# Small state products as pairs of 64-column tiles in one run, eps rows over 128 rows, tail products in pairs of chunks

## Chip, cores, metric

One core of one Trainium2 chip. The metric is device time in microseconds (us) of one execution, the median of several runs. Instruction durations are in nanoseconds (ns) where marked.

## The reference, cut to what matters

Linear attention without softmax, an RMS norm per head, then a gated feed-forward layer.

```python
# q, k, v: (8 batches, 8 heads, 576 tokens, 64); g_norm: (64,)
kv  = einsum('bhsd,bhse->bhde', k, v)        # the "state": 64x64 per head
out = einsum('bhsd,bhde->bhse', q, kv)
attn = out / sqrt(mean(out*out, -1) + 1e-6) * g_norm
x = attn as (4608, 512)
xn = x / sqrt(mean(x*x, -1) + 1e-6) * rms_g
y = (silu(xn @ w_gate) * (xn @ w_val)) @ w_out   # 512 -> 1536 -> 512
```

Almost all the work is the feed-forward layer. The change concerns the small matmuls of the attention part, which stand in the same TensorE stream.

## The kernel before

Tokens are taken in nine groups: the first 512 tokens of each of the eight batches, and the eight tails of 64 tokens together ("tails"). In a group, `up` makes one of twelve units (four gate and four value matmuls of 512 columns, then a silu on ScalarE and a product on VectorE), and `down` makes output rows. While group n is in the feed-forward layer, the small products of group n+1 are put between its units.

The state of a pair of heads, before, for batches 2 to 7: one 128x128 product holds two heads, and its two off-diagonal 64x64 blocks are never read.

```python
def kv_pair(ps, b, j, first, last):
    if b < EARLY:                       # batches 0 and 1: 64x64 tiles
        ...
                PE.matmul(ps[rows, rows], lhsT=...[rows, j, c, :], rhs=...[rows, j, c, :], ...)
        return
    hs = slice(2 * j, 2 * j + 2)        # two heads: 128 columns
    for t in range(T + 1):              # T + 1 = 5 token blocks
        PE.matmul(ps, lhsT=bufs[b]["k"][:, t, hs, :], rhs=bufs[b]["v"][:, t, hs, :],
                  start=(first and t == 0), stop=(last and t == T))

# class Att
def kv_copy(self):                      # only the diagonal blocks are copied
    SC.copy(out=kv_all[0:D, n, :, 0:D], in_=ps[0:D, :, 0:D])
    DVE.tensor_copy(out=kv_all[D:128, n, :, D:128], in_=ps[D:128, :, D:128])
def o_products(self, c, ps):
    for j in range(NS):                 # NS = 4 head pairs
        cols = ps[:, 2 * j : 2 * j + 2, :]
        if self.tail:                   # two batches' tails of 64 rows in one chunk
            for u in range(2):
                rows = slice(u * TAIL, (u + 1) * TAIL)
                PE.matmul(cols[rows], lhsT=tails_q["t"][:, c, j, rows], rhs=kv_all[:, 2 * c + u, j, :], ...)
        else: ...                       # one full matmul
```

The schedule (`SC` is ScalarE):

```python
for n in range(1, B + 1):
    ...
    if n == 1:
        steps[0] += [lambda i=i: cast_kv(2, "k", i, DVE) for i in (2, 3)]
        steps[0] += [lambda i=i: cast_kv(2, "v", i, SC) for i in (0, 1)]
        steps[1] += [lambda i=i: cast_kv(2, "v", i, SC) for i in (2, 3)]
    if n < B:
        a = atts[n + 1]
        kv0, os = (2, (4, 5, 6, 7)) if n == 1 else (0, (2, 3, 5, 6))
        if not a.tail:
            steps[kv0] += [lambda a=a: a.kv_products((0, 1))]
            steps[kv0 + 1] += [lambda a=a: a.kv_products((2, 3)), a.kv_copy]
        for c, u in enumerate(os):
            steps[u].append(lambda a=a, c=c: a.o(c))
            ...
    for unit in range(NF + T):          # 12 up-units, 4 down-units
        ffn.up(unit) ...                # or down
        for step in steps[unit]: step()
```

`att_pool` has two PSUM banks. `A`, `Z` (halves of batch 0) and `F` (batch 1) make the sums of squares on TensorE: `sums` first puts eps into the bank by matmuls of `ones` (64 rows) with `epsrow` (64 rows), then adds `sel` matmuls of 128 rows and 4 columns.

Of the kernel before, what the change touches and what calls it, by code (L numbers as in the profile page):

```python
# [10 lines left out]
FP32 = mybir.dt.float32  # L11
BF16 = mybir.dt.bfloat16
# [8 lines left out]
def kernel(  # L21
# [14 lines left out]
    B, H, S, D = q.shape  # L36
# [5 lines left out]
    T = 4  # L42
    MAIN = 128 * T
    TAIL = S - MAIN
    NS = d_model // 128
# [7 lines left out]
    def pool(name, bufs, **kw):  # L53
        return ctx.enter_context(tc.tile_pool(name=name, bufs=bufs, **kw))

    consts = pool("consts", 1)
# [17 lines left out]
    att_pool = pool("att", 2, space=PS)  # L74
# [3 lines left out]
    PE, DVE, SC, GP = nc.tensor, nc.vector, nc.scalar, nc.gpsimd  # L78
# [5 lines left out]
    gsq = consts.tile([128, 1], BF16, name="gsq")  # L84
    rowscale = consts.tile([128, NS], FP32, name="rowscale")
    sel = consts.tile([128, 2, 2], BF16, name="sel")
    ones = consts.tile([64, 128], BF16, name="ones")
    epsrow = consts.tile([64, H], BF16, name="epsrow")
    gsq8 = consts.tile([128, H, D], BF16, name="gsq8")
    kv_all = consts.tile([128, B, NS, 128], BF16, name="kv_all")  # L90
    kbs = [consts.tile([128, T + 1, H, D], BF16, name=f"kb{i}") for i in range(2)]
# [21 lines left out]
    bufs = {b: {"k": kbs[b % 2], "v": vbs[b % 2]} for b in range(B)}  # L113
# [8 lines left out]
    def pairs_buf(b, name):  # L122
        flat = bufs[b][name].rearrange("p t h d -> p (t h d)")
        return flat[:, 0 : NS * C * D].rearrange("p (j c d) -> p j c d", j=NS, c=C)
# [19 lines left out]
    def cast_kv(b, name, i, engine):  # L144

        if b < EARLY:
            cast(engine, pairs_buf(b, name)[:, i].rearrange("p c d -> p (c d)"), pairs_raw(b, name)[:, i, :])
        elif i < NS:
            hs = slice(2 * i, 2 * i + 2)
            src = raws[b, name][:, 0 : MAIN * T].rearrange("p (h t d) -> p t h d", h=H, t=T)  # L150
            cast(engine, bufs[b][name][:, 0:T, hs, :], src[:, :, hs, :])
        else:
            src = raws[b, name][0:TAIL, MAIN * T :].rearrange("r (h d) -> r h d", h=H)
            cast(engine, bufs[b][name][0:TAIL, T], src)
# [10 lines left out]
    def alloc_q(b):  # L165
        bufs[b]["q"] = qb_pool.tile([128, T, H, D], BF16, name="qb")

    def cast_q(b, hs, engine):
        src = raws[b, "q"].rearrange("p (h t d) -> p t h d", h=H, t=T)[:, :, hs, :]
        cast(engine, bufs[b]["q"][:, :, hs, :], src)  # L170

    def load_batch(b):
        load_q(b)
        for name in ("k", "v"):
            alloc_kv(b, name)
            load_kv(b, name, nc.sync)
# [85 lines left out]
    def kv_pair(ps, b, j, first, last):  # L262
        if b < EARLY:
            for c in range(C):
                for u in range(2):
                    rows = slice(u * D, u * D + D)
                    PE.matmul(
                        ps[rows, rows], lhsT=pairs_buf(b, "k")[rows, j, c, :], rhs=pairs_buf(b, "v")[rows, j, c, :],
                        start=(first and c == 0), stop=(last and c == C - 1),
                    )  # L270
            return
        hs = slice(2 * j, 2 * j + 2)
        for t in range(T + 1):
            PE.matmul(  # L274
                ps, lhsT=bufs[b]["k"][:, t, hs, :], rhs=bufs[b]["v"][:, t, hs, :],
                start=(first and t == 0), stop=(last and t == T),
            )

    def clear_tail_rows(i, engine):

# [12 lines left out]
    class Att:  # L293
        def __init__(self, n):
            self.n = n
            self.tail = n == B
            self.outa = {}
            self.xna = {}
            self.sq = {}
            self.qt = None  # L300

        def kv_products(self, js):
            if js[0] == 0:
                self.kv_ps = att_pool.tile([128, NS, 128], FP32, name="att_ps")
            for j in js:
                kv_pair(self.kv_ps[:, j, :], self.n, j, j == 0, j == NS - 1)

        def kv_copy(self):
# [38 lines left out]
                        start=(j == 0), stop=(j == NS - 1),  # L347
                    )

        def o(self, c):  # L350
            ps = att_pool.tile([128, H, D], FP32, name="att_ps")
            self.o_products(c, ps)
            self.sq[c] = sq_pool.tile([128, 2, H, D], BF16, name="sq")
            SC.activation(out=self.sq[c][:, 0], in_=ps, func=ACT.Square)  # L354
            self.outa[c] = outa_pool.tile([128, H, D], BF16, name="outa")
            SC.copy(out=self.outa[c], in_=ps)  # L356
# [247 lines left out]
    eps_hi = float(ml_dtypes.bfloat16(eps))  # L604
    eps_lo = float(ml_dtypes.bfloat16(eps - eps_hi))
# [1 line left out]
    for i in range(2):  # L607
        DVE.memset(sel[i * D : (i + 1) * D, 0, i : i + 1], 1.0 / D)
    DVE.memset(ones, 1.0)
    DVE.memset(epsrow[0:32], eps_hi / 32)  # L610
    DVE.memset(epsrow[32:64], eps_lo / 32)
    DVE.memset(kv_all[:, 0 : B - 1], 0.0)


# [35 lines left out]
    def state0(j, dummies):  # L650
        ps = att_pool.tile([128, 512], FP32, name="att_ps")
        warm(ps, max(dummies, 1), 512 if dummies else 128)
        kv_pair(ps[:, 0:128], 0, j, True, True)
        return ps
# [38 lines left out]
    kv0 = state0(0, 0)  # L693
# [60 lines left out]
    first = ffn.pair_banks()  # L754
# [79 lines left out]
    att1 = Att(1)  # L834
# [46 lines left out]
    def down_part(c, lo, hi):  # L881
        ffn.down_products(c, lo, hi, pools[c])
# [4 lines left out]

    for c in range(4):
        down_part(c, 0, 2)
    att1.kv_products((0, 1, 2, 3))  # L890
    for i, engine in enumerate((DVE, SC)):
        cast_q(1, slice(2 * i, 2 * i + 2), engine)
    att1.kv_copy()
# [48 lines left out]
    def load_q_tails():  # L942
        st = stage().rearrange("p (c x) -> p c x", c=T)
        for b in range(B):
            u = b % 2
            nc.sync.dma_start(
                out=st[u * TAIL : (u + 1) * TAIL, b // 2].rearrange("r (h d) -> r h d", h=H),
                in_=q[b, :, MAIN:S, :].rearrange("h r d -> r h d"),
            )
        tails_q["raw"] = st  # L950
        tails_q["b"] = qb_pool.tile([128, T, H, D], BF16, name="qb").rearrange("p t h d -> p t (h d)")

    def cast_q_tails(c, n, engine):
        cast(engine, tails_q["b"][:, c : c + n], tails_q["raw"][:, c : c + n])
# [12 lines left out]
    for n in range(1, B + 1):  # L967
        ffn = Ffn(n)
        steps = {u: [] for u in range(NF + T)}
        if n + 2 < B:  # L970
            steps[2].append(lambda n=n: load_batch(n + 2))
        if n == B - 3:
            load_q_tails()
# [4 lines that stand above are left out]
            steps[0] += [lambda name=name: cast_kv(2, name, NS, GP) for name in ("k", "v")]  # L978
        if n < B:
            a = atts[n + 1]  # L980
            kv0, os = (2, (4, 5, 6, 7)) if n == 1 else (0, (2, 3, 5, 6))
            if not a.tail:
                steps[kv0] += [lambda a=a: a.kv_products((0, 1))]
                steps[kv0 + 1] += [lambda a=a: a.kv_products((2, 3)), a.kv_copy]
            for c, u in enumerate(os):
                steps[u].append(lambda a=a, c=c: a.o(c))
                steps[u + 1].append(lambda a=a, c=c: a.sums(c))
            late = 2 * int(n == 1)
            steps[8 + late] += [a.head]
            steps[9 + late] += [a.guess, a.root]  # L990
            for c in range(T):
                steps[10 if c == 0 and not late else 11] += [lambda a=a, c=c: a.scale(c), lambda a=a, c=c: a.x_rows(c)]
        b = n + 2
        if b < B:
            steps[10] += [lambda b=b: alloc_q(b)]
            for i in range(2):
                steps[11] += [lambda b=b, i=i: cast_q(b, slice(4 * i, 4 * i + 4), SC)]
            for i in KV_CASTS:
                steps[12 + i // 3] += [lambda b=b, i=i: cast_kv(b, "k", i, SC)]
                steps[14 + i // 3] += [lambda b=b, i=i: cast_kv(b, "v", i, SC)]  # L1000
            for c in range(T):
                steps[13].append(lambda b=b, c=c: atts[b].q_rows(c))
        if b == B:
            for i in range(2):
                steps[11] += [lambda i=i: cast_q_tails(2 * i, 2, SC)]
            for c in range(T):
                steps[13].append(lambda c=c: turn_q_tails(c))
        for unit in range(NF + T):
            if unit < NF:
                ffn.up(unit)  # L1010
            elif n == B and unit == NF + T - 1:
                ffn.down_last(unit - NF)
            else:
                ffn.down(unit - NF)
            for step in steps[unit]:
                step()
# [30 lines left out]
```

## Time and profile before

| | |
|---|---|
| time, median of 3 runs before the change was tried | 324.51 us (324.26 to 325.29) |
| span of the profiled execution | 323.5 us |
| PE busy | 313.6 us, 97% |
| chain that ended last | 86% PE |
| waits of PE for another engine or a load | 4.1 us, all before 48 us |

From the page of before: the span, the busy times (us, share of the span, instructions), and the shares of the chain that ended last.

```profile
span 323.5 us, 5112 instructions
PE 313.6 (97%) x1893; PEld 157.0 (49%) x1927; DVE 181.2 (56%) x371; ACT 178.9 (55%) x319; POOL 20.9 (6%) x43
PE 86%; DMA 6%; DVE 4%; issue 2%; ACT 1%; DVEq 0%
```

The second line alone doesn't prove that TensorE binds, since matmuls overlap. The chain does it, with the waits, and with the starts of the matmuls: from the first up-unit of batch 1 on, but for the tails' excursions to another tile shape (below), a matmul starts one stream time after the one before it, 216 ns after 512 columns and 56 ns after 128. A nanosecond less in that stream is a nanosecond less of time.

The groups of small matmuls, by form (line, engine, operation, rows x columns of the array and output shape, count, then busy us and mean ns of one, then idle time before them):

```profile
L274 PE MATMUL att_ps<-vb,kb 128*128 128x128 bf16 x120 | 8.7, 219 | 0.0
L340 PE MATMUL att_ps<-kv_all,qt 128*64 128x128 bf16 x32 | 1.7, 225 | 0.1
L418 PE MATMUL att_ps<-epsrow,ones 64*128 64x8 bf16 x8 | 0.7, 168 | 0.1
```

The 219 ns is the span of one matmul as the profile models it, not what it costs: the timeline shows the ten of a run within 0.72 us. What counts is the distance between starts. The timeline of before on PE around batch 3's state products (start us, duration of the merged piece, what):

```profile
90.90 1.03 PE L474 MATMUL v_ps<-xnt,wv_sb 128*128 128x512 bf16 x4
91.77 0.72 PE L274 MATMUL att_ps<-vb,kb 128*128 128x128 bf16 x10
92.32 1.03 PE L474 MATMUL g_ps<-xnt,wg_sb 128*128 128x512 bf16 x4
93.19 1.03 PE L474 MATMUL v_ps<-xnt,wv_sb 128*128 128x512 bf16 x3
94.05 0.72 PE L274 MATMUL att_ps<-vb,kb 128*128 128x128 bf16 x10
```

From 91.77 to 92.32 ten full matmuls take 0.56 us, and the gate matmuls follow at once. Now the tails' output products, which use half the columns of the array (128*64):

```profile
259.81 1.03 PE L474 MATMUL v_ps<-xnt,wv_sb 128*128 128x512 bf16 x4
260.76 0.41 PE L340 MATMUL att_ps<-kv_all,qt 128*64 128x128 bf16 x8
261.11 1.04 PE L474 MATMUL g_ps<-xnt,wg_sb 128*128 128x512 bf16 x4
262.94 0.41 PE L340 MATMUL att_ps<-kv_all,qt 128*64 128x128 bf16 x8
266.84 0.41 PE L340 MATMUL att_ps<-kv_all,qt 128*64 128x128 bf16 x8
269.02 0.41 PE L340 MATMUL att_ps<-kv_all,qt 128*64 128x128 bf16 x8
```

The last of four value matmuls starts at 259.81 + 3 x 0.216 = 260.45, so the tiles could start at 260.67; they start at 260.76. The single starts of that stretch, read from the trace:

```
start us   ns after the one before
260.453    216   last 512-column matmul
260.762    309   first tile of pair 1          (+93)
260.766      4   second tile of pair 1
260.842     76   pair 2                        (24 more than the next)
260.898     52   pair 3 (56 after pair 2)
260.954     52   pair 4
260.957      3
261.109    152   512-column matmul again       (+99: 155 after pair 4, which streams 56)
261.336    227   the next                      (+11)
```

An excursion to another tile shape and back thus costs 93 + 24 + 99 + 11 = 227 ns, about 0.23 us, apart from its work.

### The profile page before, as it was taken

What the parts mean: (1) busy time and instruction counts of PE and PEld (TensorE: products, weight loads), DVE (VectorE), ACT (ScalarE), POOL (GpSimd) and SP (SyncE); (2) the same over time, 40 slices, a digit from 0 to 9 for tenths busy, and PEclk for the clock granted to TensorE, in tenths of its full rate; (3) what the DMA queues carried; (4) which work ended last, traced back from release to release, by engine and by line L of the source; (5) the groups of instructions that cost most, each with busy time, mean ns of one, the idle gap of its engine ahead of it and who ended that gap; (6) DMA issues with size and microseconds to landing.
All of it is one profiled execution on the core that took longest, in us unless ns stands there. A gap on an engine that the chain in (4) does not pass through costs nothing.

```text
span 323.5 us, 5112 instructions
## 1 busy us (share of the span) xinstructions
PE 313.6 (97%) x1893; PEld 157.0 (49%) x1927; DVE 181.2 (56%) x371; ACT 178.9 (55%) x319; POOL 20.9 (6%) x43
## 2 busy tenths in 40 slices
PE   8899999999999999999999999999999999999995
PEld 3575455554454445544544455444544444444443
DVE  4776857569427932794278516950696068703310
ACT  3686447765757476647664766566554355223321
POOL 1253351200000000000000000000000000000000
PEclk9999999999999999999999999999999999999999
DMA  7999999888369449934792377947002600240014
GB/s 264 347 351 388 377 374 292 212 245 209 62 197 299 127 130 154 316 87 97 191 330 64 65 202 187 326 90 204 1 2 49 174 38 1 47 146 6 0 34 97
DMA packets 74437, 54.87 MB, mean 170 GB/s; under 512 B 42280, under 2 KB 67116, under 8 KB 74412
## 3 DMA queue, kind: packets, MB, share of 16 engines
q1 hardware_dynamic: 74044, 53.89, 58.2%
q10 hardware_dynamic: 368, 0.66, 0.6%
q8 instruction: 15, 0.25, 0.3%
q14 instruction: 10, 0.08, 0.1%
HBM read 37.75 MB, written 9.44 MB: 146 GB/s over the span
## 4 chain that ended last, share of the span: by engine, by line
PE 86%; DMA 6%; DVE 4%; issue 2%; ACT 1%; DVEq 0%
PE v_ps L474 26%; PE o_ps L516 26%; PE g_ps L474 26%; DMA st<-in_k_dram 3%; DMA st<-in_moe_w_gate_dram 3%; PE att_ps L274 2%; PE att_ps L345 2%; DVE h_sb L480 1%; DVE ssq L363 1%; PE v_ps L516 1%; PE g_ps L516 1%; DMA out_dram<-o_sb 1%; PE o_ps L491 1%; PE att_ps L340 0%; ACT wg_sb L202 0%
## 5 line engine op out<-in xcount | busy, mean ns | idle before, releaser
L480 DVE TENSOR_TENSOR h_sb<-silu,v_ps 128x512 bf16<-128x512 bf16 x104 | 70.9, 683 | 109.5 <-ACT silu L479 68.0
L474 PE MATMUL v_ps<-xnt,wv_sb 128*128 128x512 bf16 x409 | 105.7, 379 | 0.4
L474 PE MATMUL g_ps<-xnt,wg_sb 128*128 128x512 bf16 x401 | 104.9, 379 | 0.8 <-ACT wg_sb L202 0.2
L479 ACT ACTIVATE silu<-g_ps 128x512 bf16<-128x512 f32 x104 | 62.5, 601 | 64.2 <-PE g_ps L474 52.3
L516 PE MATMUL o_ps<-wo_sb,h_sb 128*128 128x512 bf16 x386 | 87.1, 379 | 0.5
L474 PEld LDWEIGHTS <-wv_sb 128*128 128x128 bf16 x416 | 40.7, 98 | 49.1
L516 PEld LDWEIGHTS <-h_sb 128*128 128x128 bf16 x420 | 40.7, 98 | 47.7
L474 PEld LDWEIGHTS <-wg_sb 128*128 128x128 bf16 x416 | 38.7, 98 | 39.9 <-issue 0.3
L106 ACT COPY o_sb<-o_ps 128x512 f32<-128x512 f32 (+1 forms) x34 | 19.7, 580 | 38.0 <-PE o_ps L516 32.4
L363 DVE TENSOR_REDUCE ssq<-sq 128x16 f32<-128x1024 bf16 x28 | 34.2, 1220 | 1.0
L354 ACT ACTIVATE sq<-att_ps 128x512 bf16<-128x512 f32 x28 | 16.7, 597 | 13.5 <-PE att_ps L345 7.9
L106 ACT CAST vb<-st 128x512 bf16<-128x512 f32 (+2 forms) x34 | 19.5, 626 | 4.8 <-DMA st<-in_v_dram 4.8
L380 DVE TENSOR_TENSOR xna<-outa,s1y 128x512 bf16<-128x512 bf16 x28 | 17.9, 684 | 0.0
L106 ACT CAST qb<-st 128x1024 bf16<-128x1024 f32 (+1 forms) x17 | 15.4, 943 | 1.8 <-DMA st<-in_q_dram 1.8
L356 ACT CAST outa<-att_ps 128x512 bf16<-128x512 f32 x28 | 16.2, 579 | 0.0
L106 ACT CAST kb<-st 128x512 bf16<-128x512 f32 (+1 forms) x25 | 14.0, 619 | 0.0
L362 DVE TENSOR_TENSOR sq<-sq,gsq 128x512 bf16<-128x512 bf16 x28 | 11.7, 418 | 0.0
L345 PEld LDWEIGHTS <-qt 128*128 128x128 bf16 x96 | 7.4, 98 | 5.7
L345 PE MATMUL att_ps<-kv_all,qt 128*128 128x128 bf16 x96 | 9.3, 219 | 0.1
L274 PEld LDWEIGHTS <-kb 128*128 128x128 bf16 x120 | 7.7, 98 | 2.8
L617 PE MATMUL att_ps<-kv_all 128*128 128x512 bf16 (+1 forms) x21 | 7.9, 504 | 1.2 <-DVE sel L606 1.2
L274 PE MATMUL att_ps<-vb,kb 128*128 128x128 bf16 x120 | 8.7, 219 | 0.0
(139 smaller groups left out, 166.5 us busy)
## 6 DMA issues: line engine op xcount, KB each, us to landing
out_dram<-o_sb SPq DMA_DIRECT2D x14, 512.0 KB, 3.0
st<-in_q_dram SPq DMA_DIRECT2D x6, 1024.0 KB, 6.7
st<-in_k_dram SPq DMA_DIRECT2D x6, 1024.0 KB, 9.4
st<-in_v_dram SPq DMA_DIRECT2D x6, 1024.0 KB, 10.7
st<-in_moe_w_out_dram SPq DMA_DIRECT2D x6, 512.0 KB, 10.4
st<-in_moe_w_gate_dram SPq DMA_DIRECT2D x4, 512.0 KB, 8.7
st<-in_moe_w_val_dram SPq DMA_DIRECT2D x4, 512.0 KB, 9.5
st<-in_k_dram SPq DMA_DIRECT2D x4, 288.0 KB, 5.5
```

The lines of the kernel that those rows point to most:

```text
L106: engine.copy(out=dst, in_=src)
L274: PE.matmul(ps, lhsT=bufs[b]["k"][:, t, hs, :], rhs=bufs[b]["v"][:, t, hs, :], start=(first and t == 0), stop=(last and t == T),)
L345: PE.matmul(cols, lhsT=self.qt[:, j, 128 * c : 128 * c + 128], rhs=kv_all[:, self.n, j, :], start=(j == 0), stop=(j == NS - 1),)
L354: SC.activation(out=self.sq[c][:, 0], in_=ps, func=ACT.Square)
L356: SC.copy(out=self.outa[c], in_=ps)
L362: DVE.tensor_tensor(out=sq[:, 1], in0=sq[:, 0], in1=gsq8, op=OP.mult)
L363: DVE.reduce_sum(out=self.ssq[:, c], in_=sq, axis=AX.X)
L380: DVE.tensor_tensor(out=self.xna[c], in0=self.outa[c], in1=self.alpha[:, c, :].to_broadcast([128, H, D]), op=OP.mult)
L474: PE.matmul(ps, lhsT=wt[:, s, j * 128 : (j + 1) * 128], rhs=x[:, s, :], start=(s == 0), stop=(s == NS - 1),)
L479: SC.activation(out=silu, in_=g_ps, func=ACT.Silu)
L480: DVE.tensor_tensor(out=self.h[:, j, :], in0=silu, in1=v_ps, op=OP.mult)
L516: PE.matmul(self.o_ps[c], lhsT=self.h[:, j, c * 128 : (c + 1) * 128], rhs=wo_sb[:, j, :], start=(j == 0), stop=(j == NF - 1),)
```

## The change

The intent: use two 64-column tiles at once for the two heads of a pair, so that the unread off-diagonal blocks are not computed; go to the tile shape once per batch and not twice, since each change of shape costs; give the eps rows all 128 rows, so that those matmuls change no shape; and make the tails' excursions half as many.

```diff
-    ones = consts.tile([64, 128], BF16, name="ones")
-    epsrow = consts.tile([64, H], BF16, name="epsrow")
+    ones = consts.tile([128, 128], BF16, name="ones")
+    epsrow = consts.tile([128, H], BF16, name="epsrow")
 ... kv_pair, batches 2 to 7
-        hs = slice(2 * j, 2 * j + 2)
         for t in range(T + 1):
-            PE.matmul(
-                ps, lhsT=bufs[b]["k"][:, t, hs, :], rhs=bufs[b]["v"][:, t, hs, :],
-                start=(first and t == 0), stop=(last and t == T),
-            )
+            for u in range(2):
+                cols = slice(u * D, u * D + D)
+                PE.matmul(
+                    ps[cols, cols], lhsT=bufs[b]["k"][:, t, 2 * j + u, :], rhs=bufs[b]["v"][:, t, 2 * j + u, :],
+                    start=(first and t == 0), stop=(last and t == T),
+                )
 ... class Att: o(c) is cut into o_rows(cs), the products of several chunks, and put_o(c), square and copy
 ... setup
-    DVE.memset(epsrow[0:32], eps_hi / 32)
-    DVE.memset(epsrow[32:64], eps_lo / 32)
+    DVE.memset(epsrow[0:64], eps_hi / 64)
+    DVE.memset(epsrow[64:128], eps_lo / 64)
 ... schedule
-            kv0, os = (2, (4, 5, 6, 7)) if n == 1 else (0, (2, 3, 5, 6))
+            kv0, os = (3, (4, 5, 6, 7)) if n == 1 else (1, (2, 3, 5, 6))
             if not a.tail:
-                steps[kv0] += [lambda a=a: a.kv_products((0, 1))]
-                steps[kv0 + 1] += [lambda a=a: a.kv_products((2, 3)), a.kv_copy]
+                steps[kv0] += [a.kv_products, a.kv_copy]
             for c, u in enumerate(os):
-                steps[u].append(lambda a=a, c=c: a.o(c))
+                cs = ((0, 1), (), (2, 3), ())[c] if a.tail else (c,)
+                steps[u].append(lambda a=a, cs=cs: a.o_rows(cs))
+                steps[u].append(lambda a=a, c=c: a.put_o(c))
```

More of the change, by code (lines that the diff above doesn't have):

```diff
@@ L299, in __init__, with kv_products @@
             self.sq = {}
+            self.o_ps = {}
             self.qt = None
-        def kv_products(self, js):
-            if js[0] == 0:
-                self.kv_ps = att_pool.tile([128, NS, 128], FP32, name="att_ps")
-            for j in js:
+        def kv_products(self):
+            self.kv_ps = att_pool.tile([128, NS, 128], FP32, name="att_ps")
+            for j in range(NS):
                 kv_pair(self.kv_ps[:, j, :], self.n, j, j == 0, j == NS - 1)
@@ L348, in o_products, with o_rows, put_o @@
                     )
-        def o(self, c):
-            ps = att_pool.tile([128, H, D], FP32, name="att_ps")
-            self.o_products(c, ps)
+        def o_rows(self, cs):
+            for c in cs:
+                self.o_ps[c] = att_pool.tile([128, H, D], FP32, name="att_ps")
+                self.o_products(c, self.o_ps[c])
+        def put_o(self, c):
+            ps = self.o_ps[c]
             self.sq[c] = sq_pool.tile([128, 2, H, D], BF16, name="sq")
@@ L889 @@
         down_part(c, 0, 2)
-    att1.kv_products((0, 1, 2, 3))
+    att1.kv_products()
     for i, engine in enumerate((DVE, SC)):
```

## The prediction

> **What bounds the kernel now.** TensorE. The page gives PE 313.6 of 323.5 us busy (97%) and a clock digit of 9 throughout; the chain that ended last is 86% PE; the waits of PE sum to 4.1 us, all before 48 us. By start times in the timeline, from 26.7 us on almost every matmul starts one stream time after the one before: 216 ns after a 512-column matmul, 56 ns after a 128-column one. So a nanosecond taken from PE's stream after 26.7 us comes off the time; before that (loads, scale chain of the first x rows) mostly not.
>
> **What changes of array shape cost.** In the timeline a tile matmul (128x64 or 64x64) after a 512-column one starts 309 ns after it instead of 216 (+93). Going back costs about +96 ns, and +11 ns on the next matmul. The first pair of tiles is 21 ns slower. That is about 0.22 us per excursion, and agrees with the Trainium skill, "TensorEngine Tiling (Array Packing)", Key Properties: changing the tiling mode drains TensorE. Inside, the two tiles of a pair start 4 ns apart: pairs of batch 1's state products (64x64, 64 columns) come every 31.7 ns, pairs of the tails' output products (128x64, 128 columns) every 56 ns.
>
> **Costs.**
> 1. State products, batches 2 to 7. Before: two runs of 10 full matmuls per batch, 20 x 55.8 = 1.116 us, no mode change. After: 20 pairs of 64-column tiles; estimate from the 64x64 pairs: 20 x 31.7 = 0.634 us, plus 0.22 us for one excursion. Saves about 0.26 us per batch, 1.56 us over six. (In two runs it would save only 0.04 us per batch.)
> 2. Tails' output products: four excursions become two, same stream: 2 x 0.225 = 0.45 us saved.
> 3. eps rows on 128 rows: the 64-row matmuls no longer change the mode. In F (near 49 us) 512-to-sel takes 496 ns and should take 316, and 13 ns less after: 0.19 us. The sums of A and Z (13 and 17 us) are hidden: near 0.
> Other engines keep order and work. The state copy still comes one up-unit before the batch's first output products, and both att banks should be free when the chunk pairs ask for them: no new wait.
>
> All this is on the critical path: 1.56 + 0.45 + 0.19 = 2.2 us, 0.7%. Predicted: 324.5 - 2.2 = **322.3 us**, 8 in 10 between 321.3 and 323.8. Faster by over 2%: 0.01; within 2%: 0.98; slower by over 2%: 0.01.
>
> **What would show it.** Step 1: six runs of 40 matmuls 128x64, N=64, pair pitch 31.7 ns; last 512-column start to next 1.07 us (now 1.33, both runs together). Step 2: two runs of 16 tail matmuls. Step 3: 25 ns pitch from eps through sel, no steps of 90 ns. PE idle unchanged, VectorE and ScalarE groups the same.
>
> **What would make it wrong.** No trace here has a 64-column tile with 128 rows and 64 moving columns. The same page (Restrictions) says that column tiling turns Fast Weight Load off; tile loads take 106 to 110 ns here against 98. If such loads can't hide behind 27 ns of streaming and pairs come every 50 to 56 ns, step 1 costs 0.15 to 0.2 us per batch instead and the time is about 325. Also wrong: if bunching the state products makes the state copy late and PE waits at the first output products.

## More of the kernel before

Every run quoted here was with a granted TensorE clock of 0.992 to 1.0.

Lastly the sums of `F`, where the eps matmuls use 64 rows and the `sel` matmuls 128:

```profile
48.85 0.59 PE L516 MATMUL v_ps<-wo_sb,h_sb 128*128 128x512 bf16 x2
49.38 0.25 PE L418 MATMUL att_ps<-epsrow,ones 64*128 64x8 bf16 x4
49.56 0.55 PE L421 MATMUL att_ps<-sel,sqt 128*128 128x4 bf16 x16
48.91 0.69 DVE L868 TENSOR_TENSOR sqt<-o_sb,att_ps 128x512 bf16<-128x512 f32 x1
```

The last line is VectorE's square of the second head pair. It ends at 48.91 + 0.69 = 49.60, and the fifth `sel` matmul, which needs it, starts at 49.68.

## The result, and the profile after

| | before | after |
|---|---|---|
| time, median of 6 runs each | 324.49 us (324.24 to 325.32) | 322.99 us (322.42 to 323.35) |
| ratio after / before, 95% interval | | 0.9945 (0.9928 to 0.9963) |
| span of the profiled execution | 323.5 us | 321.4 us |

Ratios are the mean time of one kernel's fast runs over that of the other's of the same rounds, so not quite the ratio of the medians. 0.9945 of 324.5 us is 1.8 us less. The predicted gain was 2.2 us, and 322.99 us lies in the predicted range. The spans of the two profiled executions differ by 2.1 us, closer still to the prediction, but that is luck, as the stretches below show.

From the page of after:

```profile
span 321.4 us, 5351 instructions
PE 311.0 (97%) x2011; PEld 154.1 (48%) x2047; DVE 179.6 (56%) x371; ACT 178.8 (56%) x319; POOL 20.3 (6%) x43
PE 84%; DMA 10%; issue 1%; ACT 1%; another core or an unknown queue 1%; DVE 1%; SPq 0%; ACTq 0%
```

TensorE still binds. The small groups by form:

```profile
L275 PE MATMUL att_ps<-vb,kb 128*64 128x64 bf16 x240 | 4.9, 197 | 0.0
L341 PE MATMUL att_ps<-kv_all,qt 128*64 128x128 bf16 x32 | 1.3, 222 | 0.0
L423 PE MATMUL att_ps<-epsrow,ones 128*128 128x8 bf16 x8 | 0.6, 167 | 0.1
```

There are twice as many state products, in about half the busy time (4.9 us against 8.7), and the eps matmuls have all 128 rows. The timeline of after on PE around batch 3's state products:

```profile
92.25 1.03 PE L479 MATMUL v_ps<-xnt,wv_sb 128*128 128x512 bf16 x4
93.21 0.82 PE L275 MATMUL att_ps<-vb,kb 128*64 128x64 bf16 x40
93.96 1.04 PE L479 MATMUL g_ps<-xnt,wg_sb 128*128 128x512 bf16 x3
```

One run in place of two. Single starts of it, read from the trace:

```
start us   ns after the one before
92.896           last 512-column matmul
93.206    310    first tile of pair 1          (+94)
93.210      4    second tile
93.259     49    pair 2 (53 after pair 1)
93.291           pair 3 (32 after pair 2)
93.829           pair 20 (18 pairs after pair 2: 570 / 18 = 31.7 each)
93.831      2
93.961    130    512-column matmul again       (+100: 132 after pair 20, less 31.7)
```

From the last 512-column matmul to the next is 93.961 - 92.896 = 1.065 us, 1.07 predicted. The tails:

```profile
258.13 1.03 PE L479 MATMUL v_ps<-xnt,wv_sb 128*128 128x512 bf16 x4
259.09 0.64 PE L341 MATMUL att_ps<-kv_all,qt 128*64 128x128 bf16 x16
259.66 1.04 PE L479 MATMUL g_ps<-xnt,wg_sb 128*128 128x512 bf16 x4
264.94 0.64 PE L341 MATMUL att_ps<-kv_all,qt 128*64 128x128 bf16 x16
```

Two runs of 16, as meant. The sums of `F`:

```profile
48.31 0.59 PE L521 MATMUL v_ps<-wo_sb,h_sb 128*128 128x512 bf16 x2
48.74 0.24 PE L423 MATMUL att_ps<-epsrow,ones 128*128 128x8 bf16 x4
48.85 0.73 PE L426 MATMUL att_ps<-sel,sqt 128*128 128x4 bf16 x16
48.38 0.69 DVE L873 TENSOR_TENSOR sqt<-o_sb,att_ps 128x512 bf16<-128x512 f32 x1
```

The eps matmuls now follow the 512-column ones without a change of shape. But the `sel` matmuls take 0.73 us in place of 0.55: in the trace the fifth starts 199 ns after the fourth, at 49.12, just after VectorE's square ends at 48.38 + 0.69 = 49.07. What the eps rows gave, the wait for the square took.

And there is a wait of PE that before did not have (after, list of waits of PE: total us, times, longest):

```profile
PE g_ps L479 <- ACT silu L484: 0.3, 1, 0.3
```

To see what is systematic, I cut each trace at three instructions that all versions have: the first matmul of `F`'s columns, the first gate weight load of batch 1's up-units, and the last weight load of all. Up to the second cut is "the start", from the first to the second is "the F stretch", and from the second to the third is "the body".

| trace | start ends at, us | F stretch, us | body, us |
|---|---|---|---|
| before | 56.73 | 9.19 | 262.67 |
| after | 56.19 | 9.18 | 261.08 |

The body is 1.59 us shorter, where the prediction has 1.56 + 0.45 = 2.01. The F stretch is the same, where it has 0.19. And the start ended 0.54 us earlier, where it has nothing: by chance that made up for most of the 0.61 us that is missing in the other two.

### The profile page after: what moved, and what is told of

Same layout as the page of the kernel before. It is cut to its first block, busy times and chain, and to the rows that moved or that the text cites. A ratio compares the mean times of both kernels' runs of the same rounds, so it can differ in the third digit from the quotient of the medians.

```text
span 321.4 us, 5351 instructions
## 1 busy us (share of the span) xinstructions
PE 311.0 (97%) x2011; PEld 154.1 (48%) x2047; DVE 179.6 (56%) x371; ACT 178.8 (56%) x319; POOL 20.3 (6%) x43
## 4 chain that ended last, share of the span: by engine, by line
PE 84%; DMA 10%; issue 1%; ACT 1%; another core or an unknown queue 1%; DVE 1%; SPq 0%; ACTq 0%
PE g_ps L479 27%; PE v_ps L479 26%; PE o_ps L521 24%; DMA st<-in_v_dram 3%; DMA st<-in_moe_w_out_dram 3%; PE att_ps L346 2%; DMA gam<-in_g_norm_dram 2%; DMA st<-in_k_dram 1%; PE att_ps L275 1%; DMA out_dram<-o_sb 1%; PE g_ps L496 1%; PE o_ps L496 1%; PE v_ps L496 1%; DVE xna L460 0%
## 5 line engine op out<-in xcount | busy, mean ns | idle before, releaser
L479 PE MATMUL v_ps<-xnt,wv_sb 128*128 128x512 bf16 x405 | 104.4, 379 | 0.1
L108 POOL CAST wo_sb<-st 128x512 bf16<-128x512 f32 x12 | 7.5, 654 | 7.0 <-DMA st<-in_moe_w_out_dram 7.0
L108 DVE CAST kb<-st 128x576 bf16<-128x576 f32 (+1 forms) x12 | 5.3, 459 | 2.5 <-DMA st<-in_k_dram 2.5
```

The source lines that it names most:

```text
L108: engine.tensor_copy(out=dst, in_=src)
L479: PE.matmul(ps, lhsT=wt[:, s, j * 128 : (j + 1) * 128], rhs=x[:, s, :], start=(s == 0), stop=(s == NS - 1),)
```

## The experiments

Two theories. Theory S: each part is worth what its own stretch of TensorE's stream shows; the eps rows are worth nothing since `F`'s sums wait for VectorE; and the missing 0.42 us of the body is the one wait for a silu. Rival L: part of the gain comes from the earlier start, by the eps rows or the loads. The table gathers all runs; the sections follow. "Body" as above. Medians are of six runs, of e7 five.

| run | what it is | median us | ratio to before (95%) | start ends, us | body, us |
|---|---|---|---|---|---|
| e1_state_only | state part alone | 323.28 | 0.9946 (0.9929 to 0.9964) | 56.05 | 261.11 |
| e2_tails_only | tails part alone | 324.38 | 0.9978 (0.9957 to 0.9999) | 55.94 | 262.21 |
| e3_eps_only | eps part alone | 324.62 | 0.9991 (0.9968 to 1.0014) | 55.46 | 262.66 |
| e4_one_run_full | after, state products full size | 324.82 | 0.9988 (0.9968 to 1.0008) | 57.19 | 262.21 |
| e5_casts_later | after, batch 2's value casts later | 323.05 | 0.9947 (0.9930 to 0.9965) | 57.22 | 260.66 |
| e6_two_runs | after, tiles in two runs | 324.09 | 0.9975 (0.9956 to 0.9994) | 56.27 | 262.02 |
| e7_fill_before_sums | e5, one matmul moved | 322.39 | 0.9927 (0.9915 to 0.9939) | 55.73 | 260.66 |
| e8_after_again | after unchanged | 322.88 | 0.9938 (0.9923 to 0.9954) | 55.89 | 260.66 |
| e9_late_v | after, a later value load | 323.51 | 0.9956 (0.9939 to 0.9973) | 56.93 | 260.92 |
| e10_late_v_casts_later | e9 with the casts of e5 | 322.65 | 0.9928 (0.9910 to 0.9947) | 55.24 | 260.66 |
| e11_later_rows | e7, rows of a chunk later | 323.15 | 0.9945 (0.9924 to 0.9966) | 56.30 | 260.66 |
| e12_fill_again | e7 again | 322.73 | 0.9948 (0.9931 to 0.9966) | 55.32 | 260.66 |

The medians of before were 324.87 (e1 to e4), 324.73 (e5 to e8), 324.76 (e9 to e11) and 324.58 us (e12). All results were correct.

### Each part alone: e1, e2, e3

e1 is after with the old eps rows and with `cs = (c,)`; e2 is before with `o_rows` and `put_o` and the pairs of chunks; e3 is before with the eps lines of the diff.

```diff
 # e1, against after
-    ones = consts.tile([128, 128], BF16, name="ones")      # and epsrow, and its memsets
+    ones = consts.tile([64, 128], BF16, name="ones")
-                cs = ((0, 1), (), (2, 3), ())[c] if a.tail else (c,)
+                cs = (c,)
```

> The change with only its state-product part (64-column tiles, one run per batch); eps rows and the tails' runs as before. Theory S (each part is worth what its own stretch of the tensor engine's stream shows): six runs of 40 tile matmuls, each 0.26 us shorter than the full-size products; batch 2's 0.26 us is lost to a wait for a silu behind value casts near 61 us if the engine arrives there early, so 1.3 to 1.56 us off the before: 322.9 to 323.2 us. The tails' stretch keeps its four excursions. Rival L (the gain came from an earlier start, by loads or the eps rows): the time falls by under 0.8 us.

Measured: 0.9946 of before, about 1.75 us less by the mean, a little more than expected. Its body is 262.666 - 261.112 = 1.55 us shorter, which is 0.26 us for each of the six batches: batch 2's is not lost here, for in this trace there is no wait for a silu. Theory S holds; rival L doesn't.

> Before, with only the tails' output products in pairs of chunks. Theory S: two runs of 16 tile matmuls in place of four of 8, 0.45 to 0.49 us off: about 324.0 us, and no new wait of the tensor engine at the pairs. Rival: the pairs ask for both att banks at once and wait, so that nothing is gained.

Measured: 0.9978, 0.7 us by the mean, with an interval from almost 0 to 1.4. The trace is sharper: the body is 0.45 us shorter (262.666 - 262.212), in two runs of 16 tile matmuls, and PE has no wait there. Theory S.

> Before, with only the eps rows on 128 rows. My prediction gave this 0.19 us in F. Theory W (from the trace after: the sums now wait for VectorE's square of the second pair, which used to end only 0.07 us before its use): the steps of over 90 ns around the eps matmuls are gone, but a gap of 0.1 to 0.2 us appears after the fourth sel matmul, and under 0.05 us is gained; time within 0.2 us of before. Rival L: the eps rows bring the 0.5 us by which the trace after is ahead at 48 us; then this run is 0.4 to 0.6 us faster than before and its F stage starts at 47.5 us, not 48.2.

Measured: 0.9991, no difference that can be told. The body is 262.66, as before (262.67); the F stretch is 9.19 us, as before; the fifth `sel` matmul starts 195 ns after the fourth. So the eps rows remove the change of shape and gain nothing: theory W. But the start ended at 55.46, which looks like rival L's 0.5 us and more. It isn't, as e4 and e5 show below: they have the same eps rows, and theirs ended at 57.2. The start differs by about 2 us from trace to trace: it ended at 55.24 to 57.22 with the new eps rows (11 traces, mean 56.2) and at 55.94 to 56.73 with the old ones (3 traces, mean 56.2).

One piece of that is visible. VectorE's cast of `qb` in front of batch 1's turns took 0.43 us in after, e1, e2 and e3, but in before the GpSimd engine had begun a cast 0.01 us earlier:

```profile
44.85 2.52 POOL L108 CAST wo_sb<-st 128x512 bf16<-128x512 f32 x4 [3.16 <-DMA st<-in_moe_w_out_dram]
44.86 0.89 DVE L108 CAST qb<-st 128x512 bf16<-128x512 f32 x1
```

In after the VectorE cast came first, and took half as long:

```profile
44.72 0.43 DVE L108 CAST qb<-st 128x512 bf16<-128x512 f32 x1
45.15 1.17 POOL L108 CAST wo_sb<-st 128x512 bf16<-128x512 f32 x2 [2.95 <-DMA st<-in_moe_w_out_dram]
```

This agrees with the Trainium skill, "SBUF — State Buffer", Who interferes with whom: a VectorE cast can run in a mode that also uses a pair of ports shared with GpSimd, and whichever of the two issues first has that pair for its whole instruction. (The ports themselves no trace shows.) In e4 GpSimd was 0.01 us ahead again and the cast took 0.88 us; in e1 VectorE was 0.03 us ahead and it took 0.43. PE waited 0.4 us for this cast in the five traces in which it took 0.87 to 0.89 us (before, e4, e6, e8, e9); the lists of the others have no such wait. Which comes first hangs on when a weight load lands, and after and e8, the same program, have one case each (0.43 and 0.87 us): it is chance with respect to this change. The rest of the spread of the start I have not traced.

### Tiles or position: e4 and e6

e4 has the full-size matmuls back, in one run at the change's place. e6 keeps the tiles, in two runs.

```diff
 # e6, against after (e4: kv_pair as in before)
-                steps[kv0] += [a.kv_products, a.kv_copy]
+                steps[kv0 - 1] += [lambda a=a: a.kv_products((0, 1))]
+                steps[kv0] += [lambda a=a: a.kv_products((2, 3)), a.kv_copy]
```

> After, with the state products of batches 2 to 7 as full 128-column matmuls again, but in one run at the change's place. Theory S: 20 matmuls of 55.8 ns per batch, no change of mode, so slower than after by 5 x 0.26 = 1.3 us (1.56 if batch 2 counts), and 0.4 to 0.6 us faster than before. The wait of the tensor engine for a silu near 61 us shows here too when the engine is early, since it comes from moving the products behind a later unit, not from the tiles. Rival: tiles as such cost or gain nothing and the position does it; then this run equals after.

Measured: body 262.21, which is 1.55 us longer than the body of after without the silu wait (260.66), 0.45 shorter than before, and the same as e2's: exactly the tails. So the position gains nothing; the tiles do. The times agree: e4's ratio to before is 0.9988, after's 0.9945, and the intervals don't overlap. No wait for a silu showed: this trace's start was late, and ScalarE stood idle for the values for only 1.56 us.

> After, with the 64-column state products in two runs per batch, at the places of before. Theory S (an excursion costs 0.22 us whatever its length, a pair of tiles 31.4 ns): two excursions per batch, 20 pairs x 31.4 = 0.63 us + 2 x 0.22 = 1.07 us against 1.116 for full matmuls: about 0.04 us per batch gained over before, and 0.22 us per batch or 1.3 us in all lost to after. Rival (the drain is small when the run is short, or the gain is all in the tiles): within 0.4 us of after.

Measured: body 262.02, 1.36 us longer than 260.66, and 0.20 shorter than e4's, which is 0.03 us per batch. In time, 0.9975 against 0.9938 for after, intervals apart. From the timeline of e6 on PE, batch 3:

```profile
90.63 0.81 PE L480 MATMUL v_ps<-xnt,wv_sb 128*128 128x512 bf16 x3
91.37 0.51 PE L275 MATMUL att_ps<-vb,kb 128*64 128x64 bf16 x20
91.81 1.04 PE L480 MATMUL g_ps<-xnt,wg_sb 128*128 128x512 bf16 x4
93.64 0.51 PE L275 MATMUL att_ps<-vb,kb 128*64 128x64 bf16 x20
```

The second excursion eats nearly all that the tiles gain. So "in one run" is the part of the change that makes the other part pay, and the cost of an excursion did not depend on its length: 0.22 to 0.23 us apart from the work in runs of 8, 16, 20 and 40 tile matmuls. (A count of 3 where a gate or value product has 4 matmuls is a record missing from the trace.)

### The wait for a silu: e8, e5, e9, e10

Where the wait comes from can be read in after's timeline near 61 us:

```profile
60.33 1.14 ACT L106 CAST vb<-st 128x512 bf16<-128x512 f32 x2 [2.15 <-DMA st<-in_v_dram]
61.37 0.59 ACT L484 ACTIVATE silu<-g_ps 128x512 bf16<-128x512 f32 x1
62.01 1.02 PE L479 MATMUL g_ps<-xnt,wg_sb 128*128 128x512 bf16 x4 [0.26 <-ACT silu L484]
```

ScalarE stood idle for 2.15 us until batch 2's values had landed, then made two casts, and only then the silu of unit 1. The gate matmuls of unit 3 take the bank which that silu reads. They started 640 ns after the matmul before them, where 216 would do: 0.42 us lost. In before, ten state products stood between units 2 and 3, which gave ScalarE 0.56 us; the change moved them behind unit 3. In e3 and e6, with the state products in the old place, ScalarE stood idle for 2.00 and 2.28 us, and PE lost nothing in e3 and 0.03 us in e6.

> After unchanged, a second trace and six more times on this chip. All theories: 322.4 to 323.4 us; the state products' runs and the tails' runs as in the first trace to 0.02 us. The start (up to 48 us) differs from the first trace by up to 0.7 us, as it did between traces whose start is the same program; the wait for a silu near 61 us shows if ScalarE stood idle for the value load for over about 1.8 us, and not if less.

Measured: 322.88 us. The body is 260.66, 2.01 us shorter than before, just what steps 1 and 2 of the prediction sum to. ScalarE stood idle for 1.57 us here and PE did not wait. So the wait in the first trace is occasional.

```diff
 # e5, against after: one up-unit later, behind the silu of unit 1
-            steps[0] += [lambda i=i: cast_kv(2, "v", i, SC) for i in (0, 1)]
-            steps[1] += [lambda i=i: cast_kv(2, "v", i, SC) for i in (2, 3)]
+            steps[1] += [lambda i=i: cast_kv(2, "v", i, SC) for i in (0, 1)]
+            steps[2] += [lambda i=i: cast_kv(2, "v", i, SC) for i in (2, 3)]
```

> After, with the two pairs of value casts of batch 2 on ScalarE one up-unit later, so that the second silu no longer stands behind a cast that waits for the value load. Theory W (the wait of up to 0.4 us near 61 us comes from that order and shows only when the load lands late against the tensor engine): no wait for a silu near 61 us in the trace, batch 2's stretch gains its 0.26 us, and the median is 0 to 0.3 us under that of after again in the same call. Rival (the wait comes from moving the products, whatever ScalarE does): the wait stays.

Measured: body 260.66, no wait, but 323.05 us against 322.88 for after. This was inconclusive: the start of this trace was late (57.22), so that the values (cast from 60.78 us on) would have been in time in any order, and the times are not told apart. Hence e9, which makes the load late on purpose by a useless load before it (256 KB into a part of a stage tile that nobody reads), and e10, which has that and the later casts.

```diff
 # e9 and e10, in load_batch
+            if b == 2 and name == "v":
+                nc.sync.dma_start(out=pad[0], in_=<the first 65,536 elements of q[2], as 128 x 512>)
             load_kv(b, name, nc.sync)
```

> After, with a useless 256 KB load put between batch 2's key and value loads, so that the value load lands later. Theory W: ScalarE stands idle for the value load for over 2.2 us before its first value cast, the second silu behind it is late, and the tensor engine waits for it near 61 us for 0.3 us or more (about the idle time less 1.75 us), in this trace and in most timed runs: 0.3 to 1 us slower than after. Rival (the wait seen once was chance and has nothing to do with the load): no such wait.

Measured: ScalarE stood idle for 1.99 us, less than I expected, and the gate matmuls of unit 3 started 482 ns after the one before, 0.27 us late. The added load did not make the values later, against the start, than they were by chance in the first trace of after: the first cast began 3.97 us after the end of the start, and 4.14 there (3.56 in e8). Nor do the times show the expected loss: 0.9956 of before, against 0.9945 and 0.9938 for after, intervals overlapping. From the timeline of e9 (the wait itself is not marked in it; the start at 62.59 after the weight load at 62.11 shows it):

```profile
60.90 1.14 ACT L106 CAST vb<-st 128x512 bf16<-128x512 f32 x2 [1.99 <-DMA st<-in_v_dram]
61.95 0.59 ACT L491 ACTIVATE silu<-g_ps 128x512 bf16<-128x512 f32 x1
62.11 0.10 PEld L486 LDWEIGHTS <-wg_sb 128*128 128x128 bf16 x1
62.59 0.59 PE L486 MATMUL g_ps<-xnt,wg_sb 128*128 128x512 bf16 x2
```

The five traces with this order fit one line: idle 2.15, 1.99, 1.57, 1.56 and 1.27 us (after, e9, e8, e4, e1), PE late by 0.42, 0.27, 0, 0 and 0, about the idle time less 1.7 us.

> The same late load, with the value casts of batch 2 one up-unit later as in e5. Theory W: the second silu is ahead of the casts, so the tensor engine has no wait for a silu near 61 us although the load is as late, batch 2's products still gain their 0.26 us, and it is faster than e9 by what e9 waits, 0.3 to 1 us. Rival: the wait moves to the third silu or to the state products and the time equals e9.

Measured: no wait for a silu, body 260.66, and 322.65 us against 323.51. From the timeline of e10:

```profile
58.31 0.60 ACT L491 ACTIVATE silu<-g_ps 128x512 bf16<-128x512 f32 x1 [1.08 <-PE g_ps L486]
60.21 1.14 ACT L106 CAST vb<-st 128x512 bf16<-128x512 f32 x2 [1.31 <-DMA st<-in_v_dram]
60.64 1.03 PE L486 MATMUL g_ps<-xnt,wg_sb 128*128 128x512 bf16 x4
```

The silu of unit 1 ends at 58.91, the casts begin at 60.21, and the gate matmuls of unit 3 start on time at 60.64. In the old order that silu would have stood behind those casts, until about 61.85, when the silu of unit 2, which does stand behind them here, ended. In this trace the first cast began 4.97 us after the end of the start, later than in any other trace. In e11, with the later casts and no added load, it was 4.35 us, and PE did not wait either. This settles the cause: the order on ScalarE behind a load. How often it costs something in after, and so its mean, stays open: of the four traces with this order and no added load (after, e1, e4, e8) one shows it. The difference of e9 and e10 in time is in the expected direction, but their intervals overlap, and 0.86 us is more than one such wait; part of it will be the start.

### The F stretch: e7, e11, e12

If `F`'s sums wait 0.2 us for a square, other work can go in front of them.

```diff
 # e7, against e5
+    down_part(0, 6, 7)
     F.alloc_sums()
     F.sums()
     f_o(0)
     F.head()
     F.root()
-    down_part(0, 6, 8)
+    down_part(0, 7, 8)
     down_part(1, 6, 8)
 # e11, besides: f_o(1) goes behind down_part(2, 6, 8)
```

> e5 with one down product (0.216 us) moved from behind F's sums to before them, to give VectorE's square time to end. Theory W: the gap of 0.19 us after the fourth sel matmul is gone and does not come back later (the scaled rows are no later than now), so the stretch from F's columns to the first up-unit is 0.17 to 0.19 us shorter than in e5; total 0.15 to 0.2 us under e5, near the limit of what five rounds show. Rival (the head's chain on VectorE binds this stretch anyway): the gap moves to the turns of the scaled rows and nothing is gained.

Measured: the gap after the fourth `sel` matmul is gone, but a gap of 189 ns came up before the rows of the second chunk. The next expectation takes that for a wait for VectorE. The timeline of e7 shows another engine, ScalarE, which copies the rows of the first chunk out of `att_pool`:

```profile
49.42 0.59 ACT L106 CAST outa<-att_ps 128x512 bf16<-128x512 f32 x1 [0.88 <-PE att_ps L434]
50.06 0.38 PE L434 MATMUL att_ps<-kv_all,qt 128*128 128x128 bf16 x4
```

The semaphore that the second chunk's rows wait for is that of this copy. It ends at 50.01, 0.05 us before they start, while VectorE reads the sums for the norm until 50.21. In after, the same copy ended 77 ns before these rows started, and no gap was there: the down product that I moved had been its cover. The F stretch is 9.18 us (e8: 9.19): nothing gained. The rival was right in that, but not in its reason, since the turns of the scaled rows were no later than in after (14 and 16 ns).

> e7 with the second chunk's rows of batch 1 behind one more pair of down products. In e7 the gap of 0.19 us after the fourth sel matmul came back before those rows, which take the bank that VectorE still reads for the head. Theory B: with 0.43 us more in front of them that gap is gone, and the stretch from F's columns to the first up-unit is 0.29 us shorter than after, 0.19 shorter than e7; median 0.2 to 0.3 us under after, 322.2 to 322.6. Rival (the chain on VectorE to the scaled rows binds): the gap moves on to the turns of the scaled rows, and the stretch is no shorter than in e7.

Measured: a miss. The second chunk's rows had no gap before them, but a gap of 182 ns appeared before the rows of the last chunk, again 0.05 us after the end of a copy of ScalarE, that of the second chunk's rows, which it now had later. Then the second scaled row came 226 ns late to its turn, from VectorE, and the F stretch became 9.41 us. The last part may be chance: two of the small VectorE instructions of the chain took 0.37 and 0.53 us here, and 0.18 and 0.20 in e7, while GpSimd cast weights. So no one chain is shown to bind this stretch. It stays at 9.18 to 9.19 us in the other traces because different losses there have nearly the same size: the changes of shape in before (0.19 us), VectorE's square in after, e3 and e8 (0.18 to 0.19), ScalarE's copy in e7 and e12 (0.19). An order without any of them was not found.

> e7 again, to see whether its lead over after (0.9927 against 0.9938 of before, intervals overlapping) repeats. Theory: casts later take away an occasional wait of up to 0.4 us and the moved down product is worth 0.1 us, so 0.1 to 0.3 us under after: ratio to before 0.992 to 0.9935. Rival (start jitter only): 0.9935 to 0.9955.

Measured: 0.9948, in the rival's range. The lead of e7 did not repeat. Body and F stretch of e7 and e12 are alike to 0.01 us, so the lead was probably the start's chance; the timed runs don't show their stretches. No version here is shown to beat after. e5's order is the one to keep, for it takes away an occasional loss, but no timed pair proves a gain.

## Why the prediction was right

The time and the range were right. Its steps:

- **State products, right to a few ns.** The pairs came every 31.7 ns, and 1.065 us lay between the 512-column matmuls, 1.07 predicted. e1 gives 1.55 us over six batches, 1.56 predicted. The fear that loads of tiles can't hide (the Trainium skill, "TensorEngine Tiling (Array Packing)", Restrictions: column tiling turns Fast Weight Load off) did not come true: a tile's load took 113 ns in after against 98 for a full one, and was hidden all the same.
- **Only "in one run" pays, right.** e6: two runs gain 0.03 us per batch; the prediction said 0.04.
- **Tails, right.** e2: 0.45 us; 0.45 predicted.
- **"In F (near 49 us) 512-to-sel takes 496 ns and should take 316 ... 0.19 us", wrong.** The gap of the eps rows went as said, and 0.00 us came of it (e3). "All this is on the critical path" is the sentence that failed: those gaps of TensorE lay beside VectorE's square, which ended 0.07 us before its use already in before. I had counted PE's gaps and not asked what the next instructions wait for. This is 0.19 of the predicted 2.2 us.
- **"No new wait", wrong in some executions.** The state copy was in time, as I said. The new wait is elsewhere: the products that I moved had been cover for a silu behind late casts. It took 0.42 us in the first trace and none in the second.
- **The start.** I credited it with nothing. On the whole that is right, but it varies by about 2 us between traces, as much as the whole effect, so the 0.54 us by which the first trace of after was ahead at the start is no gain of the change. That the two profiled spans differ by 2.1 us, nearly the 2.2 predicted, is luck: 1.59 of the body and 0.54 of the start.

So the sum is 1.554 + 0.454 = 2.01 us less an occasional wait, and the timed ratios, 0.9945 and 0.9938 of about 324.6 us, are 1.8 and 2.0 us.

## What to carry to other kernels

Cost a change of tile shape as a fixed price per excursion (here 0.22 to 0.23 us, the in-and-out of TensorE), and do small-tile work in few, long runs. Before you credit a gap on the busiest engine, ask what the next instruction would then wait for: a gap beside another engine's chain is worth nothing. When you move filler work, look at what it covered: here a silu behind a load, and in e7 a copy of rows on ScalarE; and when two traces differ, cut them at common instructions, since a chance start can be as large as the effect.

## What the Trainium skill lacked or had wrong

- "TensorEngine Tiling (Array Packing)", Key Properties, says that a change of mode drains TensorE, but not what it costs. Here: +92 to 94 ns in, 20 to 25 ns on the first pair, +98 to 101 ns out, +9 to 11 ns on the next matmul, 0.22 to 0.23 us in all, whether the run has 8, 16, 20 or 40 matmuls.
- "TensorE: Matmul & The Clock Gate", Wait — 56ns, not 53.3ns?, says that start-to-start never drops below about 25 ns. That agrees with the `sel` matmuls here (25 ns), but not with tiles: the two of a pair start 2 to 4 ns apart, and a pair of 64-column tiles comes every 31.7 ns, 16 ns per matmul. (Its Part 3 has the 4 ns, without this rate.)
- The same page, The mechanism (of Part 3), says, as seen in traces, that weight loads overlap with matmuls in flight only when the row group differs, though it also names a background weight buffer. Here the loads of the next 128-row pair start 1 to 2 ns after a matmul of the same rows has started, and the pairs keep their 31.7 ns with loads that the profile shows as 113 ns each.
